# Softmax weights of two heads normalized by one two-tensor multiplication instead of two multiplications with a scalar per row

## The chip, the cores and the metric

The kernel runs on one core of a Trainium2 chip. The metric is the device time of one execution in microseconds (us); three executions of the kernel before are given, and their median counts. The engines are named as in the profile: PE is TensorE (matmuls; PEld its weight loads), DVE is VectorE, ACT is ScalarE, POOL is GpSimd, SP is SyncE (here it issues most DMAs).

## What is computed

The reference is windowed attention followed by two feed-forward stages. For the edit the first matters: scores of each head with a distance bias, a mask (96 local and 8 global positions), a softmax over the row, and the product with the values.

```python
scores = scale * np.matmul(q, k.transpose(0, 1, 3, 2))      # B, H, S, D = 2, 8, 768, 64
scores = scores + bias[None, :, :, :]
scores = np.where(keep, scores, -1000000000.0)
scores = scores - np.max(scores, axis=-1, keepdims=True)
a = np.exp(scores)
a = a / (np.sum(a, axis=-1, keepdims=True) + 1e-09)          # the division that the edit touches
attn = np.matmul(a, v)
h = x @ w_in                                                 # x: 1536 x 512, w_in: 512 x 2048
g = np.where(h > 0.0, h, np.exp(np.minimum(h, 0.0)) - 1.0)
x = g @ w_out
h = np.maximum(np.maximum(x @ w1, x @ w2), x @ w3)           # 512 x 768 each
out = h @ w_out2
```

## The kernel before

**Attention steps.** A step is 128 queries of two heads (`u` = 0, 1, one on each half of PE's rows). There are 48 steps: 6 groups of 256 queries, 4 pairs of heads, 2 halves of a group (`t`). A step sees only a window of keys: 232 columns (96 + 8 + 128), or 128 where it is the first block of a sequence (8 of the 48 steps). The row tile `p` (128 x 512, f32) holds both heads side by side: head 0 in columns 0 to n, head 1 from column 232 on, with n = 232 or 128. The small tile `m` (128 x 8) holds for each head the row's extreme (columns 0, 1), the sum (2, 3), the sum plus 1e-9 (4, 5) and its reciprocal (6, 7).

Step k passes through these stages, each a method called from the loops: `scores_pe` (PE, L217), `scores_dve` (DVE adds the bias and finds the extreme, L243, a custom instruction and the reading of its accumulator for each head), `scores_act` (ACT's exponential with a row sum, L264), `sums` (ACT, L226), `recip` (DVE, L255), `norm` (DVE, L277, the method that is edited), `turn_pe` (PE transposes p in four pieces of 116 columns, or two of 128: L293, L287), `turn_act` (the copy of the transposed tile out of PSUM, L304), `values_pe` (PE, L316), and then a copy or a split of the result (L326, L332, or L352).

**The order of the work** is written out by hand: the queues of the engines run in the order in which the Python loops issue, and semaphores order them against one another. Three parts matter.

- *The head* (`windowed`): steps 0 to 17, one loop turn each. In turn k the order is: scores on PE for k, values for k-3, transposes for k-2; DVE's bias for k; ACT's copies for k-3 and k-2 and exponentials for k, then the sums; DVE's reciprocal and `norm` for k-1; DVE's split remainder (L332) for k-3. From turn 7 on pieces of the conversion of the first weights are put in behind (`c_low` L408, `c_word` L415, `c_rest` L428 on DVE; `c_rebase` L404, `c_high` L423 on ACT): the weights come as 64-bit floats, whose words are put together into an f32, which is split into a rounded part and a remainder.
- *The first feed-forward stage* (`Feed.run`): three blocks of 512 tokens, 16 turns each. A turn multiplies the block with one slice of w_in (`product`, L505, 12 matmuls), takes the activation (ACT L525, L526, DVE L530), splits it (ACT L512; remainder L517 on POOL in block 0, on DVE later) and multiplies with the slice of w_out before (L536, L544). The other 30 attention steps are put into the turns of blocks 0 and 1, one each: PE does the transposes of step k-1 right behind `product`, and on even k then the scores of k and k+1. DVE does `scores_dve`, later `recip` and `norm` of step k. In block 0 the conversion of the next slices of weights stands between these, so `norm` follows a `c_word` (L415) and is followed by `c_rest` (L428).
- *The second stage* (L700 on): three products and a maximum (L725) and the output rows (L569, L574, L579), without attention.

At the change of blocks `run` splits the next tokens (L485 on ACT, L486 on DVE) and saves the finished block (L558).

Of the kernel before, what the change touches and what calls it, by code (L numbers as in the profile page):

```python
# [17 lines left out]
ALU = mybir.AluOpType  # L18
# [5 lines left out]
P = 128  # L24
# [8 lines left out]
WIN = PREV + G + P  # L33
# [75 lines left out]
class Windowed:  # L109
# [159 lines left out]
    def norm(self, k):  # L269
        if k not in self.p_t:  # L270
            return
        nc = self.nc
        n = self.geom(k)[-1]
        p, m = self.p_t[k]
        for u in range(2):
            o = slice(u * WIN, u * WIN + n)
            nc.vector.tensor_scalar(p[:, o], p[:, o], m[:, 6 + u:7 + u], None, op0=ALU.mult)  # L277

    def turn_pe(self, k, tag="TX"):
        if k not in self.p_t:  # L280
# [756 lines left out]
```

## Time and profile before

| | |
|---|---|
| three runs | 569.98, 570.61, 571.79 us, median 570.61 |
| span of the profiled execution, first to last instruction | 569.0 us |
| PE busy | 549.6 us (97%) |
| DVE busy | 315.4 us (55%) |
| ACT busy | 277.1 us (49%) |
| POOL busy | 78.3 us (14%) |
| `norm` (L277), 96 instructions | 28.3 us of DVE |

The span leaves out what the device does ahead of the first instruction and behind the last, so it is a little shorter than a run's time. Busy shares are means over the whole span; the stages have different limits, and a stretch has to be read by itself. A start in the timeline is when the instruction began on its engine; the next one can begin a little before the one ahead has ended, since an engine's pipeline overlaps them. In brackets behind an instruction stands how long its engine had been idle, and what the profile takes for the releaser. "Issue" there means that nothing the profile shows was waited for.

### The profile page before, as it was taken

The page shows a single profiled execution, that of the slowest core. Times are in us where ns is not written, and L with a number is a line of the kernel's source. Part 1 is how long each engine was busy: PE and PEld are TensorE (multiplying, and loading weights), DVE is VectorE, ACT ScalarE, POOL GpSimd, SP SyncE. Part 2 cuts the span into 40 slices and gives each one's busy share as a digit, 9 for nine tenths or more (in the row PEclk, how much of TensorE's full clock was granted, in tenths as well). Part 3 has the DMA queues.
Part 4 walks back from the last instruction along what each step waited for, and adds up shares of the span by engine and source line. Part 5 has one row for each costly group of instructions (what it writes and reads, how often), then busy time and mean ns, then how long its engine had stood idle before and what let it go on. Part 6 is the DMA issues. An engine that isn't in the chain of part 4 may idle for free. (4 is left out here: it accounts for less than half of the span.)

```text
span 569.0 us, 7586 instructions
## 1 busy us (share of the span) xinstructions
PE 549.6 (97%) x2772; PEld 435.0 (76%) x2772; DVE 315.4 (55%) x684; ACT 277.1 (49%) x622; POOL 78.3 (14%) x87
## 2 busy tenths in 40 slices
PE   8799999999999999999999999999999999999995
PEld 6467777776777777778888888888887888888884
DVE  6987999999745333333466656567754112312112
ACT  5988777777656555554555554524323101311011
POOL 4100222222210000000011222023320000000000
PEclk9969999999999999999999999999999999999999
DMA  8919444532211111010013223122302000010002
GB/s 293 381 45 345 166 168 137 181 122 78 67 36 42 42 41 43 20 55 1 0 38 111 88 98 111 37 75 77 117 29 75 1 1 0 8 67 1 0 1 79
DMA packets 16669, 46.61 MB, mean 82 GB/s; under 512 B 1776, under 2 KB 1776, under 8 KB 16624
## 3 DMA queue, kind: packets, MB, share of 16 engines
q1 hardware_dynamic: 15760, 44.47, 22.8%
q10 hardware_dynamic: 864, 1.57, 0.8%
q8 instruction: 24, 0.39, 0.3%
q14 instruction: 21, 0.17, 0.1%
HBM read 42.90 MB, written 3.15 MB: 81 GB/s over the span
## 5 line engine op out<-in xcount | busy, mean ns | idle before, releaser
L505 PE MATMUL h<-xh,w 128*128 128x512 f32 (+1 forms) x536 | 144.5, 391 | 0.8 <-ACT xh L485 0.8
L505 PEld LDWEIGHTS h<-xh,w 128*128 128x128 f32 x536 | 98.1, 188 | 24.5 <-issue 1.8
L536 PE MATMUL y<-gh,w 128*128 128x512 f32 x384 | 98.6, 399 | 0.0
L512 ACT CAST gh<-e 128x512 fp32r<-128x512 f32 x66 | 41.0, 622 | 101.8 <-DVE e L725 87.4
L536 PEld LDWEIGHTS y<-gh,w 128*128 128x128 f32 x384 | 69.7, 188 | 18.1 <-ACT e L526 1.7
L725 DVE TENSOR_TENSOR e<-S,e 128x512 f32<-128x512 f32 x36 | 24.9, 692 | 103.5 <-PE S L505 100.8
L505 PE MATMUL h<-xl,w 128*128 128x512 f32 (+1 forms) x268 | 81.8, 386 | 0.0
L505 PE MATMUL S<-xh,w 128*128 128x512 f32 x288 | 77.0, 389 | 0.0
L530 DVE SCALAR_TENSOR_TENSOR e<-e,h 128x512 f32<-128x512 f32 x48 | 33.0, 687 | 67.7 <-ACT e L526 67.7
L505 PEld LDWEIGHTS S<-xh,w 128*128 128x128 f32 x288 | 54.1, 188 | 11.2
L525 ACT ACTIVATE e<-h 128x512 f32<-128x512 f32 x48 | 28.7, 597 | 65.2 <-PE h L505 63.0
L462 POOL TENSOR_TENSOR w<-wr,w 128x512 fp32r<-128x512 f32 x24 | 35.4, 1474 | 166.1 <-ACT w L461 166.1
L505 PEld LDWEIGHTS h<-xl,w 128*128 128x128 f32 x268 | 50.0, 188 | 10.3
L517 DVE TENSOR_TENSOR gl<-e,gh 128x512 fp32r<-128x512 f32 x50 | 39.8, 796 | 31.8 <-ACT gh L512 31.6
L264 ACT ACTIVATE p<-p,m 128x232 f32<-128x232 f32 (+1 forms) x96 | 44.8, 469 | 24.4 <-DVE m L243 24.4
L544 PE MATMUL y<-gl,w 128*128 128x512 f32 x192 | 51.5, 390 | 0.0
L415 DVE SCALAR_TENSOR_TENSOR wr<-wr 128x1024 uint32<-128x1024 uint32 (+1 forms) x36 | 49.9, 1395 | 0.8 <-ACT wr L404 0.2
L505 PE MATMUL S<-xl,w 128*128 128x512 f32 x144 | 44.3, 389 | 0.0
L451 DVE SCALAR_TENSOR_TENSOR wr<-wr 128x512 uint32<-128x512 uint32 x48 | 43.0, 896 | 2.2
L544 PEld LDWEIGHTS y<-gl,w 128*128 128x128 f32 x192 | 36.0, 188 | 7.9 <-issue 0.3
L569 PE MATMUL y<-w,gh 128*128 128x512 f32 x144 | 37.3, 390 | 0.4 <-POOLq L941 0.4
L517 POOL TENSOR_TENSOR gl<-e,gh 128x512 fp32r<-128x512 f32 x16 | 21.0, 1310 | 104.3 <-ACT gh L512 104.3
(85 smaller groups left out, 604.4 us busy)
## 6 DMA issues: line engine op xcount, KB each, us to landing
wr<-wa SPq DMA_DIRECT2D x14, 1024.0 KB, 6.4
wr<-wb SPq DMA_DIRECT2D x24, 512.0 KB, 3.3
v<-v SPq DMA_DIRECT2D x24, 256.0 KB, 2.8
raw<-qk SPq DMA_DIRECT2D x16, 312.0 KB, 3.1
raw<-qk SPq DMA_DIRECT2D x8, 260.0 KB, 3.3
wr<-wa SPq DMA_DIRECT2D x4, 512.0 KB, 3.8
out<-ot ACTq DMA_DIRECT2D x6, 256.0 KB, 2.6
out<-ot SPq DMA_DIRECT2D x6, 256.0 KB, 2.5
```

The costliest lines, as they stand in the source:

```text
L264: self.nc.scalar.activation(p[:, o], p[:, o], AF.Exp, bias=m[:, u:u + 1], scale=-1.0, accum_out=m[:, 2 + u:3 + u],)
L415: self.nc.vector.scalar_tensor_tensor(r[..., 0], r[..., 1], v, r[..., 0], op0=op, op1=ALU.bitwise_or)
L451: self.nc.vector.scalar_tensor_tensor(t, a, c, t, op0=op, op1=ALU.bitwise_or)
L462: nc.gpsimd.tensor_tensor(w[:, j % 2, 1], v, w[:, j % 2, 0].bitcast(F32), op=ALU.subtract)
L505: nc.tensor.matmul(out[:, o:n], w[:, part % 2, c * P:c * P + P], (xl if part == 2 else xh)[:, c, o:n], start=c == 0 and part == 0, stop=c ...
L512: self.nc.scalar.copy(gh[:, 0:n], e[:, 0:n])
L517: (engine or self.nc.vector).tensor_tensor(gl[:, 0:n], e[:, 0:n], gh[:, 0:n].bitcast(F32), op=ALU.subtract)
L525: self.nc.scalar.activation(e, h, AF.Relu, scale=-1.0)
L530: self.nc.vector.scalar_tensor_tensor(e, e, -1.0, h, op0=ALU.add, op1=ALU.max)
L536: self.nc.tensor.matmul(y[e][:, 0:n], w[:, a, e * P:e * P + P], g[0][:, 0:n], start=fc == 0 and a == 0, stop=False,)
L544: self.nc.tensor.matmul(y[e][:, 0:n], w[:, 0, e * P:e * P + P], g[1][:, 0:n], start=False, stop=fc == NFC - 1,)
L569: nc.tensor.matmul(o[r], gh[:, r * P:r * P + P], w[:, a], start=j == 0 and a == 0, stop=False,)
```

## The change

`norm` no longer multiplies each head's n columns by a scalar per row (the reciprocal of that head in column 6 or 7 of `m`). It makes a view q of p, 128 x 2 x n, over both heads, and a view r of the two reciprocals in which each is repeated n times by a stride of zero, and multiplies q by r in place with one instruction of two tensors. For n = 232 the two heads adjoin, so that q is one run of 464 columns; for n = 128 a gap of 104 columns lies between them.

```diff
     def norm(self, k):
         ...
         p, m = self.p_t[k]
-        for u in range(2):
-            o = slice(u * WIN, u * WIN + n)
-            nc.vector.tensor_scalar(p[:, o], p[:, o], m[:, 6 + u:7 + u], None, op0=ALU.mult)
+        q = p[:, 0:2 * WIN].rearrange("p (u c) -> p u c", u=2)[:, :, 0:n]
+        r = m[:, 6:8].unsqueeze(2).to_broadcast([P, 2, n])
+        nc.vector.tensor_tensor(q, q, r, op=ALU.mult)
```

No other instruction is added, removed or moved on any engine. What the joined instruction changes besides itself is what PE waits for. PE's queue in the head of the program, at step 3 (turn 5), before (the names: y, S and TX are PSUM tiles, raw holds queries and keys, v the values, ident an identity matrix):

```order
L316 MATMUL y_246<-p,v 64x128 [waits DMAHW6_49,Activation_49]
L316 MATMUL y_246<-p,v 64x128
L293 MATMUL y_268<-ident,p 116x128 [waits DVE_49,PE_49]
L293 MATMUL y_268<-ident,p 116x128
L293 MATMUL y_268<-ident,p 116x128 [waits DVE_49]
L293 MATMUL y_268<-ident,p 116x128
L217 MATMUL S_293<-raw 128x128 [waits DMAHW5_49,Pool_49]
```

And the same place of the changed kernel:

```order
L316 MATMUL y_243<-p,v 64x128 [waits DMAHW6_49,Activation_49]
L316 MATMUL y_243<-p,v 64x128
L293 MATMUL y_264<-ident,p 116x128 [waits DVE_49,PE_49]
L293 MATMUL y_264<-ident,p 116x128 x3
L217 MATMUL S_288<-raw 128x128 [waits DMAHW5_49,Pool_49]
```

Before, the first and the third transpose of a step each waited for DVE, that is for the multiplication of head 0 and of head 1. Now the first alone waits, for the one multiplication of both heads.

## Rows read from the trace of the kernel before

**Rows 1.** The page: busy time of each engine, and PE's granted clock in 40 slices

```profile
PE 549.6 (97%) x2772; PEld 435.0 (76%) x2772; DVE 315.4 (55%) x684; ACT 277.1 (49%) x622; POOL 78.3 (14%) x87
...
PEclk9969999999999999999999999999999999999999
```

**Rows 2.** Busy time by stretch: PE, PEld, DVE, ACT, POOL, clock, DMA share, GB/s

```profile
11.13:14.44 3.31, 3.06 (x28) 1.83 (x30) 2.76 (x19) 3.25 (x15) 0.48 (x1) 1.00 1.04 414
14.44:17.74 3.30, 3.05 (x28) 1.82 (x30) 2.76 (x17) 3.23 (x16) 0.00 (x0) 1.00 1.03 389
60.00:150.00 90.00, 86.12 (x466) 64.90 (x464) 82.87 (x155) 70.00 (x144) 24.47 (x19) 1.00 0.38 128
...
180.00:563.00 383.00, 382.23 (x1796) 311.12 (x1795) 168.15 (x306) 142.02 (x283) 37.37 (x28) 1.00 0.13 44
```

**Rows 3.** Groups of DVE by shape: busy us, mean ns, idle before

```profile
L277 DVE TENSOR_SCALAR p<-p,m 128x232 f32<-128x232 f32 x80 | 24.3, 345 | 1.4
...
L486 DVE TENSOR_TENSOR xl<-xraw,xh 128x512 fp32r<-128x512 f32 x8 | 5.2, 686 | 0.2 <-ACT xh L485 0.2
...
L277 DVE TENSOR_SCALAR p<-p,m 128x128 f32<-128x128 f32 x16 | 4.0, 293 | 0.3
...
L157 DVE TENSOR_TENSOR sc<-sc,rel 128x360 f32<-128x360 f32 x1 | 0.5, 526 | 0.0
```

**Rows 4.** Who waited for L277, us in total and times

```profile
  PE TX L293: 3.9, 7
```

**Rows 5.** Timeline of the head: start us, length us, instruction, count

```profile
12.65 0.20 ACT L226 ACTIVATE m<-m 128x2 f32<-128x2 f32 x1
...
13.09 0.59 DVE L277 TENSOR_SCALAR p<-p,m 128x232 f32<-128x232 f32 x2
...
13.60 0.28 DVE L332 TENSOR_TENSOR xl<-TX,xh 128x128 fp32r<-128x128 f32 x1
...
13.71 0.65 PE L293 MATMUL y<-ident,p 128*116 128x128 f32 x4
...
14.39 0.58 ACT L304 COPY p<-y 116x512 f32<-116x512 f32 x1
...
15.96 0.20 ACT L226 ACTIVATE m<-m 128x2 f32<-128x2 f32 x1
```

**Rows 6.** Timeline of the first block, two turns from 84 to 100 us

```profile
88.03 1.96 DVE L415 SCALAR_TENSOR_TENSOR wr<-wr 128x1024 uint32<-128x1024 uint32 x1
...
90.09 0.61 DVE L277 TENSOR_SCALAR p<-p,m 128x232 f32<-128x232 f32 x2
90.58 0.41 PEld L293 LDWEIGHTS TX<-ident,p 128*116 128x116 f32 x4 [0.82 <-issue]
90.61 0.62 PE L293 MATMUL TX<-ident,p 128*116 128x128 f32 x4 [0.42 <-DVE p L277]
...
91.18 1.23 DVE L428 TENSOR_TENSOR w<-wr,w 128x1024 fp32r<-128x1024 f32 x1 [0.47 <-ACT w L423]
...
98.57 0.39 PE L505 MATMUL h<-xl,w 128*128 128x512 f32 x1
...
99.61 0.62 ACT L525 ACTIVATE e<-h 128x512 f32<-128x512 f32 x1
```

**Rows 7.** Timelines of DVE and of PE from 126 to 166 us

```profile
129.45 1.23 DVE L415 SCALAR_TENSOR_TENSOR wr<-wr 128x1024 uint32<-128x1024 uint32 x1
...
149.48 0.62 PE L293 MATMUL TX<-ident,p 128*116 128x128 f32 x4 [0.50 <-DVE p L277]
```

**Rows 8.** Timeline of the change to the second block, 163 to 184 us

```profile
163.29 1.89 DVE L486 TENSOR_TENSOR xl<-xraw,xh 128x512 fp32r<-128x512 f32 x3
...
172.01 1.41 DVE L558 COPY yraw<-y 128x256 f32<-128x256 f32 x4
...
179.37 0.59 DVE L277 TENSOR_SCALAR p<-p,m 128x232 f32<-128x232 f32 x2
179.83 0.41 PEld L293 LDWEIGHTS TX<-ident,p 128*116 128x116 f32 x4 [1.06 <-ACT e L525]
```

## The prediction

> **What bounds the kernel now.** I read the page's busy shares and slices first, then busy time by stretch, then the groups of VectorE (DVE) by shape, and last the timeline around each place where TensorE (PE) waits for a normalized tile. PE is busy 97% of a span of 569.0 us [rows 1]; its matmuls set the end in most of the program. Three stretches differ, and the edit acts in the first two alone. From 180 us on PE is busy 382.23 of 383.00 us [rows 2]: nothing that DVE does there reaches the end while DVE stays ahead. From 60 to 150 us (the first block, where weights are converted beside the matmuls) PE is busy 86.12 and DVE 82.87 of 90.00 us [rows 2]: both are near full, so the waits must be read one by one. In the head (8 to 48 us, attention steps one behind the other) a pair of steps takes 3.30 us, in which ACT is busy 3.23 [rows 2].
>
> The work that is edited is small: 80 multiplications of 128x232 at 345 ns and 16 of 128x128 at 293 ns, 28.3 us of DVE in all [rows 3]. PE's waits on it are listed as 3.9 us in 7 cases [rows 4], and another wait of the same kind, at 179.83, is put down to ACT (below).
>
> **How the old pair behaves.** In the head the pair starts at 13.09, and the next DVE instruction starts at 13.60 [rows 5]: the pair holds DVE for 0.51 us, though each half lasts 0.34, because the second starts before the first has ended. PE does not wait for both halves. Its first weight load for the transposes starts 0.49 us after the pair (90.09 to 90.58), before the pair's end at 0.61 [rows 6]: it was released by head 0 alone. That is 0.34 for the first half and some 0.14 of latency.
>
> **What the joined multiplication costs.** The trace has no TENSOR_TENSOR of 464 elements, and none with a stride of zero; both sides must be bounded. The nearest rows are TENSOR_TENSORs with f32 inputs in SBUF: 128x360 in 526 ns, 128x512 in 686 ns [rows 3], so 1.05 ns for an element more. At 464 this gives 526 + 104 x 1.05 ns = 0.64 us, and at 256 (the steps with 128 columns a head) 0.42 us. A chained TENSOR_TENSOR holds DVE for some 0.09 us less than it lasts (three of 128x512 in a row take 1.89 us together, so 0.60 each between starts, against 0.69 [rows 8, 3]). So the joined one holds DVE for 0.55 us where the pair held it 0.51: 0.04 more in each of 40 steps, and at 256 elements 0.34 against about 0.40 (0.51 less the two shares of 0.05 by which its halves are shorter), 0.06 less in 8 steps. From below: were it to run at the rate of the TENSOR_SCALARs (345 - 293 = 52 ns for 104 elements, 0.5 ns each [rows 3]), it would last about 0.46 us. From above: were the zero stride read at half rate, about 1.1 us. I take 0.64, since a strided row near it is not slow: a SCALAR_TENSOR_TENSOR of 128x1024 that reads every second word takes 1.23 us [rows 7], which the line through the rows of 360 and 512 gives for 1024 elements too (0.69 + 512 x 1.05 ns).
>
> The Trainium skill ("VectorE: DVE Perf Modes", Rules for kernel authors) advises for chained DVE operations: "Minimize op *count*, not sems". By that rule the merge should give something back in each step; by the rows a TENSOR_TENSOR needs twice the time for an element, and this eats what the saved start gives. With the rule alone the DVE term of the sum below would be below nothing instead of 0.1 us; the latency term, which is the larger, would stay.
>
> The larger cost is **latency for PE**: all four transposes now need the joined result. The first weight load can start 0.64 + 0.14 = 0.78 us after the multiplication starts, not 0.49: **0.29 us later wherever PE stands waiting for it**. The third transpose no longer waits by itself; since the four of a step stand 0.11 us apart without a gap when PE is late (from 149.48, 0.62 us for four [rows 7]), that wait costs nothing now and gives nothing.
>
> **Where it reaches the end.**
> (a) Head, 8 to 20 us. Here a loop closes: ACT's sums at 12.65, DVE's reciprocal, pair 13.09, transposes 13.71 to 14.36, ACT's copy 14.39, exponentials from 14.88, next sums of this kind 15.96: 3.31 us [rows 5]. The transposes start 0.62 after the pair; with 0.78 they start 0.16 later, and ACT's copy, which starts as they end, too. There are three such turns before 20 us: 3 x 0.16 = 0.5 us. The steps with 128 columns between them have slack and take nothing.
> (b) Head, 20 to 28 us: weights are converted beside the steps, DVE has no idle time, and two pairs lie on its path before ACT waits for it: 2 x 0.04 = 0.1 us. From 28 to 48 us PE (at the lower clock for about ten us [rows 1]) and ACT set the pace, and the later multiplications are covered by ACT's copies and PE's queue. Without that cover it would be another 6 x 0.04 = 0.2 us.
> (c) First block. DVE and ACT close a loop of their own: DVE's word-building at 88.03 to 89.99, then ACT's rounding L423, then DVE's remainder L428 at 91.18, which waits 0.47 us for ACT [rows 6]. The pair at 90.09 lies in that gap: 0.04 us more is hidden. PE waits 0.42 us for the pair, and will start 0.29 later; but PE's next product ends at 98.96, while ACT's relu of it starts at 99.61, behind ACT's own L404 [rows 6]. So 0.65 us of slack takes the 0.29, and as PE is held to DVE's beat at the next wait, it isn't added up. Cost inside the block: 0.
> (d) Last wait of this block, 149.48 (0.50 us) [rows 7]: behind it PE runs ahead of DVE and ACT, so that its delay stays: +0.3 us.
> (e) The turn to the second block. Here the pair lies right ahead of DVE's four copies at 172.01, behind which the remainder follows that ACT's next tile waits for [rows 8]: +0.04. Then the pair at 179.37 releases PE's weight load at 179.83, 0.46 later, the same signature as above; the view names ACT there (1.06 us), by the nearest event [rows 8]: +0.3 us. After this PE waits for no DVE result on its chain.
>
> Sum: 0.5 + 0.1 + 0 + 0.3 + 0.04 + 0.3 = **1.2 us**. The span of 569.0 becomes 570.2; the median of the runs shown is 570.61, 1.6 us above the span (start and end around it), so the forecast is 571.8 us, +0.2%.
>
> **Rivals.**
> 1. *Absorbed.* ACT in the head may have more slack than the 0.03 us between the transposes' end and its copy, and (d) or (e) may be caught by a later wait of PE for ACT. Then 0.1 to 0.5 us are left: 570.9. For it: many waits of ACT between 20 and 30 us; against: each place was followed to its successor.
> 2. *Carried (slower).* In the first block PE is busy 86.12 of 90.00 us [rows 2] and waits for just this tile in every second iteration, 7 times. If PE were the bound there, each delay would add: 7 x 0.29 = 2.0 us, of which (d) is one, so 1.2 + 1.7 = 2.9 us: 573.5, +0.5%. It decides when the slack of ACT behind PE's product (0.65 us at 99.61) is less than the delay, so from a joined multiplication of about 1.0 us, or if the slack is smaller in the other turns. For it: PE's share; against: no DVE or ACT instruction of that block is put down to PE in its wait.
> 3. *Zero stride read at half rate*: 1.1 us, DVE held 0.5 longer a step. Loop (a) loses 3 x 0.6, (b) 2 x 0.5, (d) and (e) 0.75 each, and DVE in the block begins to exceed the 0.47 us of cover: about +5 to +7 us, 576.5.
> 4. *The clock.* PE's granted clock falls to its lower level (1.2 of 2.4 GHz) for about ten us, in the third slice (28 to 43 us) [rows 1]; ahead of it PE stood idle for more of the time than anywhere later. A slower head leaves PE idle a little more; a second such stretch costs at most half its length, 5 us (574 to 576); if the first moved or went away, up to 3 us would come back (569).
> 5. *The edit brings nothing faster than before by itself.* The best case of the multiplication, 0.46 us, would save DVE 0.1 us in the few steps where DVE is the path, and still delay PE by 0.1 at the others: 570.4.
>
> **How the numbers follow.** A difference of 0.3% (1.7 us) is about what a measurement of this kernel can tell from none. Chances: forecast 0.50 (571.0 to 572.8), absorbed, with 5, 0.22 (570.3 to 571.1), carried 0.15, half rate 0.05, clock 0.08 (0.05 slower, 0.03 faster). Slower by over 0.3% (above 572.3): a quarter of the forecast's own half, most of carried, and the slower parts of 3 and 4: 0.34. Faster (below 568.9): 0.03, rounded to 0.04. Within: 0.62. The range leaves out the faster clock, half rate and a second fall: 570.2 to 573.6.
>
> **What would show it.** The joined row at 0.62 to 0.66 us for 464 elements and 0.41 to 0.44 for 256; PE's first transposes 0.77 us after it wherever PE waits; a pair of head steps at 3.45 instead of 3.30 us; the beat of the first block unchanged (PE's waits at 90.61 and 149.48 lie 58.87 us apart [rows 6, 7]), with PE's waits there no shorter than before; PE's last busy stretch shifted by 1.2 us and equally long. Wrong it would be if the joined row lasted over 0.8 us, if the first block became longer, or if the clock's low stretch had another length.

## The result and the profile after

| | median | runs | spread |
|---|---|---|---|
| before | 570.48 us | 4 | 569.98 to 571.79 |
| changed | 577.32 us | 4 | 573.59 to 580.83 |

The ratio is 1.011 with an interval of 1.0068 to 1.0153: the change is slower, by more than the measurement is uncertain, and the time lies above the predicted range. Twelve more runs of the changed kernel, beside 35 of the kernel before, gave 574.71 against 570.42 us, ratio 1.007 (1.0038 to 1.0101). The changed kernel's runs scatter: the two of them that were traced (578.74 here, 580.15 in experiment 4) show different courses of PE's clock in the first 45 us. A time alone therefore mixes the edit with the clock, and most of what follows compares the start of the same instruction in two traces.

The page of the changed kernel, the lines that answer to [rows 1]:

```profile
PE 553.2 (96%) x2772; PEld 437.2 (76%) x2772; DVE 318.3 (55%) x636; ACT 277.9 (48%) x622; POOL 78.9 (14%) x87
...
PEclk8679999999999999999999999999999999999998
```

PE is busy 3.6 us longer for the same 2772 matmuls. That is the clock: the second slice (14 to 29 us) stands at 6, where before it stood at 9. (With the same course of the clock, in experiment 7, PE is busy 548.0 us with either form.) The groups of DVE, which answer to [rows 3], and PE's waits on L277, which answer to [rows 4]:

```profile
L277 DVE TENSOR_TENSOR p<-p,m 128x464 f32<-128x464 f32 x40 | 26.8, 671 | 1.4
...
L277 DVE TENSOR_TENSOR p<-p,m 128x256 f32<-128x256 f32 x8 | 3.4, 426 | 0.3
```

```profile
  PE TX L293: 7.9, 16
```

DVE spends 1.9 us more on it (30.2 for 28.3). PE's listed waits grow from 3.9 us in 7 cases to 7.9 in 16. To see where the end moved, I took the start of each attention step's first DVE instruction (L243) in both traces, and the difference:

| place | before, us | changed - before |
|---|---|---|
| step 4 (head) | 11.91 | +0.42 |
| step 6 | 15.23 | +2.26 |
| step 10 | 24.75 | +4.21 |
| step 18 (into the first block) | 51.16 | +4.19 |
| step 32 (end of the first block) | 151.41 | +4.39 |
| step 33 | 160.82 | +4.67 |
| step 35 | 177.41 | +4.74 |
| step 39 (second block) | 206.03 | +5.32 |
| step 43 | 234.62 | +5.89 |
| step 47 | 263.21 | +6.47 |
| last output copy ends | 563.30 | +6.73 |

There are three places: the head between 12 and 24 us, the end of the first block (+0.3), and the second block, which loses some 0.14 us a step from 177 us on. In the head the clock does it. Busy time by stretch (columns as in [rows 2]) of the changed kernel:

```profile
8.00:12.00 4.00, 2.79 (x19) 1.78 (x18) 3.41 (x17) 3.48 (x16) 1.45 (x2) 0.84 1.03 399
12.00:16.00 4.00, 4.00 (x24) 2.20 (x22) 2.39 (x13) 3.22 (x14) 0.48 (x1) 0.50 1.04 410
16.00:20.00 4.00, 4.00 (x22) 2.34 (x20) 2.08 (x9) 2.83 (x11) 0.71 (x2) 0.50 1.05 398
20.00:24.00 4.00, 4.00 (x23) 2.29 (x21) 3.00 (x14) 2.85 (x11) 0.42 (x2) 0.50 0.61 232
```

From 12 to 24 us the clock is 0.50, the lower level (1.2 GHz), where before it was 1.00 [rows 2]; by the trace's clock records it is low from 10.74 to 24.4 us. Now PE is busy all of each stretch, where before 28 matmuls filled 3.06 of 3.31 us [rows 2]: PE has become the bound of the head. The timeline there:

```profile
15.62 1.11 PE L293 MATMUL y<-ident,p 128*116 128x128 f32 x4
...
16.76 0.59 ACT L304 COPY p<-y 116x512 f32<-116x512 f32 x1 [0.76 <-PE y L293]
```

Four transposes take 1.11 us (0.65 in [rows 5]) and ACT waits for them. The low stretch costs some 3.7 us: the 4.21 us at step 10 less about 0.5 that the edit itself costs there (experiment 7). Before, one of 10 us lay at 30.3 to 40.6 us, and the changed kernel has one of 6.8 us there too (34.6 to 41.5), so this is an additional one.

The first block keeps its beat. Its timeline, which answers to [rows 6, 7]:

```profile
94.45 0.73 DVE L277 TENSOR_TENSOR p<-p,m 128x464 f32<-128x464 f32 x1
...
95.29 0.41 PEld L293 LDWEIGHTS TX<-ident,p 128*116 128x116 f32 x4 [0.77 <-issue]
95.32 0.62 PE L293 MATMUL TX<-ident,p 128*116 128x128 f32 x4 [0.38 <-DVE p L277]
...
154.16 0.62 PE L293 MATMUL TX<-ident,p 128*116 128x128 f32 x4 [0.51 <-DVE p L277]
```

From 95.32 to 154.16 are 58.84 us; before, the same two transposes stood 58.87 apart [rows 6, 7]. The second block does not keep it. First the timeline of the kernel before:

```profile
193.68 0.59 DVE L277 TENSOR_SCALAR p<-p,m 128x232 f32<-128x232 f32 x2
...
194.14 0.41 PEld L293 LDWEIGHTS TX<-ident,p 128*116 128x116 f32 x4 [0.26 <-issue]
194.17 0.62 PE L293 MATMUL TX<-ident,p 128*116 128x128 f32 x4
...
208.47 0.62 PE L293 MATMUL TX<-ident,p 128*116 128x128 f32 x4
```

And the same place of the changed kernel:

```profile
198.52 0.17 DVE L255 RECIPROCAL m<-m 128x2 f32<-128x2 f32 x1 [1.04 <-ACT m L226]
198.72 0.64 DVE L277 TENSOR_TENSOR p<-p,m 128x464 f32<-128x464 f32 x1
...
199.48 0.41 PEld L293 LDWEIGHTS TX<-ident,p 128*116 128x116 f32 x4 [0.56 <-issue]
199.51 0.62 PE L293 MATMUL TX<-ident,p 128*116 128x128 f32 x4 [0.17 <-DVE p L277]
...
214.09 0.62 PE L293 MATMUL TX<-ident,p 128*116 128x128 f32 x4 [0.16 <-DVE p L277]
...
272.42 0.62 PE L293 MATMUL TX<-ident,p 128*116 128x128 f32 x4 [0.17 <-DVE p L277]
```

PE now waits for the joined result in every second turn, six times between 199 and 273 us, and from one such turn to the next are 14.58 us (199.51 to 214.09) where there were 14.30 (194.17 to 208.47). **The sign of it stood in the trace of before**: the weight load started 0.46 us after the pair, as at 179.83 [rows 8], only with a gap of 0.26 us that the view calls "issue". PE took head 0 there just as it came. With the joined form the load starts 0.76 after the multiplication (198.72 to 199.48), and the loop through PE's product, ACT's relu (L525, L526), DVE (L530), ACT (L512), DVE (L517, L243), ACT's exponentials and sums, and DVE's reciprocal returns each 0.28 to the next turn, as experiment 4 tests.

### The profile page after: what moved, and what is told of

The parts are those of the page before. It is cut to its first block, busy times and chain, and to the rows that moved or that the text cites. A ratio compares the mean times of both kernels' runs of the same rounds, so it can differ in the third digit from the quotient of the medians.

```text
span 576.8 us, 7547 instructions
## 1 busy us (share of the span) xinstructions
PE 553.2 (96%) x2772; PEld 437.2 (76%) x2772; DVE 318.3 (55%) x636; ACT 277.9 (48%) x622; POOL 78.9 (14%) x87
## 5 line engine op out<-in xcount | busy, mean ns | idle before, releaser
L512 ACT CAST gh<-e 128x512 fp32r<-128x512 f32 x66 | 41.0, 622 | 101.4 <-DVE e L725 87.1
L530 DVE SCALAR_TENSOR_TENSOR e<-e,h 128x512 f32<-128x512 f32 x48 | 33.0, 687 | 69.3 <-ACT e L526 69.3
L525 ACT ACTIVATE e<-h 128x512 f32<-128x512 f32 x48 | 28.6, 597 | 65.4 <-PE h L505 63.1
L517 DVE TENSOR_TENSOR gl<-e,gh 128x512 fp32r<-128x512 f32 x50 | 39.7, 795 | 31.8 <-ACT gh L512 31.6
L415 DVE SCALAR_TENSOR_TENSOR wr<-wr 128x1024 uint32<-128x1024 uint32 (+1 forms) x36 | 49.9, 1396 | 0.7
L517 POOL TENSOR_TENSOR gl<-e,gh 128x512 fp32r<-128x512 f32 x16 | 21.0, 1313 | 106.9 <-ACT gh L512 100.9
```

What stands on the lines that cost most here:

```text
L415: self.nc.vector.scalar_tensor_tensor(r[..., 0], r[..., 1], v, r[..., 0], op0=op, op1=ALU.bitwise_or)
L512: self.nc.scalar.copy(gh[:, 0:n], e[:, 0:n])
L517: (engine or self.nc.vector).tensor_tensor(gl[:, 0:n], e[:, 0:n], gh[:, 0:n].bitcast(F32), op=ALU.subtract)
L525: self.nc.scalar.activation(e, h, AF.Relu, scale=-1.0)
L530: self.nc.vector.scalar_tensor_tensor(e, e, -1.0, h, op0=ALU.add, op1=ALU.max)
```

## The experiments

Three explanations are to be told apart. **Theory A**: latency. All transposes wait for the whole result, and each place at which PE took head 0 just in time loses 0.28 us, in the second block in every second turn. **Rival B**: DVE's own time, 642 ns for a pair that held it 0.51. **Rival C**: the clock alone; the edit itself costs about the predicted 1.2 us. The expectations, written before the runs, use one name otherwise: their "theory B" is that the earlier fall of the clock is chance at the start of the program and not the edit's doing, while their theory A counts it as the edit's. That question is taken up in experiment 6.

**1. The joined form in the head alone, and behind it alone.** In the first kernel it is used in the 18 steps of the head:

```diff
-        for u in range(2):
+        if k < 18:
...
+            nc.vector.tensor_tensor(q, q, r, op=ALU.mult)
+        else:
+            for u in range(2):
```

> Joined multiplication in steps 0 to 17 (the head), the pair in steps 18 to 47. Theory A (what the traces before and after suggest: PE's first transposes start 0.3 us later at each place where they wait, which costs about 0.5 us in the head, 0.3 at the end of block 0 and 6 x 0.28 = 1.7 us in block 1; the rest of the loss is PE's clock, which falls in the first turns of the head because PE then stands idle longer): 571.0 us without any more time at the lower clock, and up to 577 with it, scattered over more than 2 us from run to run; two turns of block 1 take 14.30 us as before. Theory B (the earlier fall of the clock is chance at the start of the program, not the edit): 571 us, with clock and scatter of the kernel before (569.98 to 571.79).

Measured: 571.61 us (12 runs, 569.96 to 576.43), ratio 1.0039 (1.0009 to 1.0069). In the trace it is 0.46 to 0.56 us behind the kernel before from step 10 to step 14, near the sum of (a) and (b) of the prediction; from step 16 on it is 0.83 to 0.90 ahead, since the clock did not fall after it had risen (0.82 at the end). So the low stretch of before (30.3 to 40.6 us) costs about 1.4 us. The scatter does not tell the two views of the clock apart: 28 runs of the kernel before, beside it, went from 568.34 to 577.16 us. The second block, with its pairs, has the old beat.

The second kernel is the reverse (`if k >= 18`).

> The pair in steps 0 to 17, the joined multiplication in steps 18 to 47. Theory A: 570.5 + 0.3 + 0.3 + 1.7 = 572.8 us, within 0.8 us from run to run, mean clock 0.989 as before; two turns of block 1 take 14.58 instead of 14.30 us. Theory B: the clock and the scatter of the changed kernel (573.6 to 580.8) in some runs, whatever the head does.

Measured: 574.05 us (11 runs, 571.76 to 580.42), ratio 1.0071 (1.0035 to 1.0106). Against the trace of before: +0.05 at step 31, +0.40 at step 33, +0.44 at step 35, +1.00 at step 39, +2.15 at step 47, +2.47 at the last copy. With the head untouched the loss of the blocks is there, and the second block holds 2.0 of it. Rival C falls: the blocks cost more than twice the whole sum of the prediction, although the low stretch of the clock was shorter than before (6.8 us for 10.2). Two things were not as expected: the median lies 1.2 us above the 572.8, and the runs scatter over 8.7 us instead of 0.8. Runs that far above the others thus come also with the pair in the head.

**2. Head 1 first.** The pair stays, in reverse order, so that DVE's work is the same but the first transposes need the second result:

```diff
-        for u in range(2):
+        for u in (1, 0):
```

> The pair everywhere, but head 1 is multiplied ahead of head 0, so that PE's first transposes wait for the second multiplication, 0.25 us later, while DVE works no longer than before. Theory A (it is the latency): like the changed kernel, 570.5 + 0.4 + 0.3 + 0.2 + 6 x 0.22 = 572.7 us and above it with the clock, up to 579; PE's waits for L277 16 or more instead of 7. Rival (it is the time that DVE is held, or the two-tensor form): 570.5 us as before.

Measured: 574.02 us (12 runs, 572.91 to 579.29), ratio 1.0075 (1.0046 to 1.0105); +0.27 at step 33, +1.23 at step 43, +2.00 at the end, with 14.54 us from turn to turn. Its timeline in the second block:

```profile
194.18 0.59 DVE L277 TENSOR_SCALAR p<-p,m 128x232 f32<-128x232 f32 x2
...
194.89 0.41 PEld L293 LDWEIGHTS TX<-ident,p 128*116 128x116 f32 x4 [0.51 <-issue]
```

The load starts 0.71 after the pair instead of 0.46. No multiplication was joined, and the loss of the second block came back but for 0.04 us in every second turn. This tells A from B: it is when head 0 is ready, not what DVE does. (The view lists 10 waits of PE for L277 here, 6.5 us, not the 16 that were expected; it is the beat that shows the loss.)

**3. More idle matmuls in the head**, to hold the clock: nine of the first steps get four matmuls that nobody uses.

```diff
-FILL = 2, 2
+FILL = 9, 4
```

> The joined multiplication everywhere, and in the first 9 turns of the head 4 idle matmuls on the identity a turn (before: 2 in each of the first 2 turns), to keep PE at work. Theory A: the clock doesn't fall before 20 us, or less often; 570.5 + 2.9 = 573.4 us or up to 1 us more for the idle matmuls, scatter below 2 us, mean clock 0.989 or more. Theory B: like the changed kernel, 573.6 to 580.8.

Measured: 577.35 us (5 runs, 577.14 to 578.45), ratio 1.012 (1.0076 to 1.0164). That is 4 us above the 573.4 that were expected. The five runs do not scatter and the trace's first low stretch starts at 34.88 us, but the filling stands in PE's path (+3.3 us at step 7, at full clock). As a cure it fails. That the scatter of the changed kernel is the clock's fits this, but five runs are too few to show it, since of the changed kernel's 16 runs only four lie over 3.5 us above its fastest.

**4. The changed kernel again, and the second block's loop made shorter.** First the changed kernel as it is.

> The changed kernel once more, beside the kernel before on the same chip, for its scatter. Theory A (+0.5 us in the head, +2.4 us from 149 us on, and in some runs 3.7 us for an earlier stretch at the lower clock): the fastest runs at 572.5 to 573.5, the median 573 to 575, and single runs up to 581. Rival (the first four runs show what the edit always costs): median 577, none below 573.5.

Measured: 574.71 us (12 runs, 573.70 to 580.15). The median is where theory A expected it, so the 577.32 us of the first four runs are not what the edit always costs. The profiled run was the one of 580.15, and it shows a clock that came late. A row of its timeline, and a stretch of busy time:

```profile
17.00 1.11 PE L293 MATMUL y<-ident,p 128*116 128x128 f32 x4
```

```profile
16.00:20.00 4.00, 4.00 (x25) 2.39 (x22) 1.99 (x12) 2.81 (x13) 0.96 (x2) 1.00 1.02 381
```

The transposes run at half speed (1.11 us) and PE is busy throughout, though the clock column says 1.00: the trace has no clock record before 23.96 us, and without one the view shows full speed.

Next, if A holds, anything that starts the loop's end earlier takes the loss away. In the second block DVE's work for the next scores (L243, in `scores_dve`) goes ahead of the remainder (L517, in `low`); once with the pair, once with the joined form:

```diff
+                if late and bi:
+                    at.scores_dve(k)
                 gl = self.low(e, gh, n, nc.gpsimd if bi == 0 else nc.vector)
-                if late:
+                if late and not bi:
                     at.scores_dve(k)
```

> The pair, but in block 1 DVE adds the bias (L243) ahead of the remainder (L517), so that exponentials, sums, reciprocal and multiplication come about 1 us earlier in each turn. Theory A (in block 1 PE's transposes in every second turn start just as the pair is done, with 0.26 us of idle weight load ahead): PE no longer waits there, 6 or 7 x 0.1 to 0.26 = 0.7 to 1.8 us less: 568.3 to 569.4. Rival (PE sets the pace in block 1, and the pair has slack): no difference, 570.0.

> The joined multiplication with the same earlier bias in block 1. Theory A: block 1 takes as long as with the pair in this order, so 0.5 (head) + 0.3 (end of block 0) + 0.1 = 0.9 us more than with the pair, some 569.2 to 570.3 in the fast runs, 2 to 3 us below the changed kernel; two turns of block 1 take the same time with pair and joined. Rival (the loss in block 1 has another cause than when the tile is ready): 1.7 us or more above the pair in this order.

Measured: 568.99 us with the pair, ratio 0.998 (0.9951 to 1.0009), and 570.90 with the joined form, ratio 1.0017 (0.9979 to 1.0055), 12 runs each. The two traces have the same course of the clock. The joined one is 1.34 us behind at step 32, 1.59 at step 33 and 1.63 at steps 36, 39, 43, 47 and at the last copy: **the second block's loss is gone**, and the rest remains. Why, shows the timeline of the joined one:

```profile
192.60 0.64 DVE L277 TENSOR_TENSOR p<-p,m 128x464 f32<-128x464 f32 x1
...
194.01 0.40 PE L505 MATMUL h<-xl,w 128*128 128x512 f32 x1
194.02 0.59 PEld L293 LDWEIGHTS TX<-ident,p 128*116 128x116 f32 x4
```

The result is there 0.78 us before PE gets to it (193.24 to 194.02), and both kernels go from turn to turn in 14.24 us. That is 0.06 us less than the pair needed in the old order (14.30), so even the pair had nothing to spare there. The rest, 1.63 us, is more than the 0.9 that were expected; 1.11 of it lie ahead of step 18.

**5. The filling made small.** Two idle matmuls a step in steps 8 to 12 too, with the pair and the loop of experiment 4:

```diff
-            if k < FILL[0]:
+            if k < FILL[0] or 8 <= k < 13:
                 f.fill(at.ident, FILL[1])
```

> The pair with the earlier bias of block 1, and two idle matmuls a turn in turns 8 to 12 of the head, where PE stands idle for 1 to 2 us a turn (18 to 30 us). If PE's idle time there is what lets the clock fall at 30 us, that stretch goes: 1.4 us less than the pair in this order, 567 to 568, mean clock 0.995 or more. If not, the same as the pair in this order or up to 1 us slower.

> Joined multiplication with the earlier bias of block 1 and the idle matmuls in turns 8 to 12, beside the same with the pair (568.0 us median, 567.4 the fastest). Theory A: the head's and the block borders' 1.6 us stay: fastest 569.0, median 569.6 to 570; low stretch of the clock at 30 us gone or shorter. Rival (the head's loss is only the clock's): 568.0.

Measured: 568.01 us with the pair, ratio 0.9958 (0.9924 to 0.9992), and 569.66 with the joined form, ratio 0.9991 (0.9957 to 1.0025). The joined form's median stays 1.7 us behind, as in experiment 4 (1.9); the two traces differ in their clock, so they do not settle where. Two runs of the pair and four of the joined form lie 4 to 6 us above the fastest. Three of these six have a granted clock of 0.982 to 0.985 on record, the other three 0.998 and 0.999, as a late clock without a record, like that of the 580.15 above, would leave it. So three more idle matmuls go ahead of the first step (`WARM = 11` for 8), with the pair:

> The pair with the earlier bias, the idle matmuls in turns 8 to 12, and 11 instead of 8 idle matmuls at the start of the program. If the slowest runs (5 us above the others) are those in which PE's clock stays low from the start to 24 us, and more work at the start lets it rise, they go: 567.4 to 569 us in all runs. If not: 568.0 us with 1 or 2 of 12 runs near 573, as with 8.

Measured: 567.95 us, ratio 0.9932 (0.9903 to 0.9962), all 12 runs within 567.47 to 569.04. **This one beats both kernels.** Its clock on the page:

```profile
PEclk9999999999999999999999999999999999999998
```

**6. Does the joined form bring the late clock?** The joined form in the eight steps of 128 columns alone (`if n == P`), the first step among them, where PE's first transposes now come at 9.4 instead of 8.9 us.

> The joined multiplication in the 8 steps with 128 columns a head alone, the pair in the other 40. Where PE waits it waits for tiles of 232 columns, except once at 8.9 us. Theory A: 0 to 0.2 us more than before, 570.4 us, DVE 0.06 us less busy in each of the 8 steps; block 1 at 14.30 us for two turns. Rival (the form with a stride of zero costs more than its rows show, wherever it stands): 0.5 us or more above before.

Measured: five of 12 runs at 570.4 to 572.0 us, near the 570.4 expected, and seven at 575.0 to 577.8, which were not expected; median 575.35, ratio 1.0056 (1.0018 to 1.0093). In its profiled run (571.47) all blocks stand 0.3 us ahead of before, but its low stretch of the clock is the shorter one (6.8 for 10.2 us); beside the pair of experiment 7, at the same course of the clock, it is 0.2 to 0.4 us behind from step 14 on. Read with the others: of the kernels with eight idle matmuls at the start and the joined form in the head, 23 of 64 runs lie over 3.5 us above the fastest of their kernel, of those with the pair 31 of 164. Experiment 3's filled kernel is left out of this (none of 5); without the kernel of this experiment it is 16 of 52. That would suit an edit that raises the chance of a late clock, but the kernel before has such runs too (22 of 117), the shares of single kernels go from 2 in 12 to 7 in 12, and most of these runs were not traced. It **stays open** whether the edit raises the chance.

**7. Both forms at an equal clock.** The eleven idle matmuls, once with the joined form, once with the pair, and nothing else:

```diff
-WARM = 8
+WARM = 11
```

> The changed kernel with 11 instead of 8 idle matmuls at the start, nothing else. If the changed kernel's runs of 577 to 581 us are those in which PE's clock is low for most of the first 24 us, and the idle matmuls let it rise in time: 573.5 to 575 us in 11 or 12 of 12 runs, median 574.3, so 3.5 to 4.2 us above the pair with the same start. If the edit brings on the low clock whatever stands ahead: 2 to 5 of 12 runs stay above 577.

> The kernel before with 11 instead of 8 idle matmuls at the start. Median 570.2 us, and none of its runs at 573 to 577, where one in five of the kernel before lies; the difference to the changed kernel with the same start is then the cost of the edit without the clock's chance: 0.6 in the head, 0.4 + 0.3 at the block borders, 2.1 in block 1, 3.4 us in sum (theory A); 1.2 us if block 1 is as the prediction had it.

Measured: 574.97 us joined (10 runs, 573.41 to 577.01), 570.18 with the pair (12 runs, 568.95 to 571.70); ratios 1.0072 (1.0041 to 1.0103) and 0.9996 (0.9974 to 1.0018). The pair came out as expected. The joined form's median is 0.7 us above its expectation, and five of its ten runs lie above the 575 that all but one were to stay below. In the two traces the clock has the same course, with one low stretch of 6.8 us from 28.4 and from 28.6 us. So their difference up to the last output copy is the edit:

| place | joined - pair, us | gained there |
|---|---|---|
| step 10 | +0.44 | head |
| step 18 | +0.65 | head, 0.65 in all |
| step 21 | +0.94 | first block, once |
| step 31 | +0.97 | first block, 0.32 in all |
| step 33 | +1.32 | last wait of the first block, 0.35 |
| first transposes of the second block, 180 us | +1.67 | 0.35 |
| last ones of it, 268 us | +3.34 | six further turns, 1.67 |
| last output copy | +3.36 | nothing from 268 us on |

Rows behind the last three lines, of the pair:

```profile
179.26 0.63 PE L293 MATMUL TX<-ident,p 128*116 128x128 f32 x4 [0.69 <-ACT e L525]
...
562.14 0.58 ACT L745 COPY ot<-y 128x512 f32<-128x512 f32 x1 [0.77 <-PE y L574]
```

And of the joined form:

```profile
180.93 0.62 PE L293 MATMUL TX<-ident,p 128*116 128x128 f32 x4 [0.97 <-DVE p L277]
...
268.42 0.62 PE L293 MATMUL TX<-ident,p 128*116 128x128 f32 x4 [0.16 <-DVE p L277]
...
565.50 0.59 ACT L745 COPY ot<-y 128x512 f32<-128x512 f32 x1 [0.77 <-PE y L574]
```

The spans differ by 4.4 us (568.1 and 572.5), of which about 1.0 lies behind the last output copy. That stretch is 5.0 us long in one kernel with the joined form (experiment 1, head), 5.8 in another (experiment 4), 6.4 to 6.8 in the changed kernel and here, and 6.6 with the reversed pair of experiment 2, so it does not go with the joined form alone. Where it comes from is not settled.

## Why the prediction was wrong

**The price of the instruction: right.** The joined row has a median of 642 ns for 464 elements and 426 for 256; 0.64 and 0.42 were predicted. It holds DVE for 0.56 us (9.86 to 10.42 us in experiment 7's joined trace; 0.55 predicted). A stride of zero costs nothing that shows here, and rival 3 falls. The strided row that the prediction leaned on was a weak support, though: L415 of 128x1024 takes 1.23 us in one place [rows 7] and 1.96 in another [rows 6].

**The latency: right, but for the first block.** In the head and the second block PE's first weight load starts 0.76 us after the multiplication (0.78 predicted), 0.30 later than behind the pair. Where PE waits in the first block it starts 0.84 after (94.45 to 95.29), 0.36 later than behind the pair: these rows last 0.73 us instead of 0.64. All seven of them in experiment 7's joined trace overlap one of POOL's multiplications (L187).

**(a) and (b), the head: the sum is near, its parts are not.** At equal clock it is 0.65 us against 0.6 (experiment 7). Of this 0.47 is there by step 11, at 27 us. It then shrinks to 0.38 at step 17, and the rest comes from PE's waits at 46 and 48 us, where the prediction counted on cover: the transposes start 0.79 us after the multiplication there, and 0.49 after the pair. That the parts add up to the forecast is in part luck, and in experiment 4 the head costs 1.11 us.

**(c), the first block: nearly.** The beat is unchanged, but the block took 0.32 us once, nearly all of it at one turn near its start; "0" was wrong by that. The timeline of the joined form of experiment 7:

```profile
69.03 1.18 ACT L404 ACTIVATE wr<-wr 128x1024 f32<-128x1024 f32 x1
...
69.59 0.39 PE L505 MATMUL h<-xl,w 128*128 128x512 f32 x1
...
70.36 0.60 ACT L525 ACTIVATE e<-h 128x512 f32<-128x512 f32 x1 [0.15 <-issue]
...
71.73 0.69 DVE L530 SCALAR_TENSOR_TENSOR e<-e,h 128x512 f32<-128x512 f32 x1 [0.27 <-ACT e L526]
```

The same place with the pair (experiment 7):

```profile
68.57 0.39 PE L505 MATMUL h<-xl,w 128*128 128x512 f32 x1
...
69.44 0.59 ACT L525 ACTIVATE e<-h 128x512 f32<-128x512 f32 x1
```

With the joined form ACT is idle ahead of its relu for 0.15 us, and DVE then waits 0.27 us for ACT; in the pair's trace neither gap is there. The relu starts 0.38 us after PE's product has ended (69.98 to 70.36); with the pair it is 0.48 (68.96 to 69.44), behind ACT's L404. So this turn took up 0.10 of the 0.36 us and passed the rest on. The prediction had read 0.65 us of slack at 99.61 [rows 6] and let it stand for all turns. Why the relu did not start sooner is not shown: in the next such turns of the same trace it starts 0.16 to 0.48 us after the product (from 85.03 to 85.19 in the first), the delay is taken up, and the block runs on DVE's beat again. Rival 2 had named this case, a slack that is smaller in other turns.

**(d), the last wait of the first block: right**, 0.35 us (0.3 predicted). **(e), the first wait of the second block: right** too, 0.35 us, and the signature of 0.46 us was rightly read as head 0, against the releaser that the view named.

**The step that failed is the last sentence of (e)**: "After this PE waits for no DVE result on its chain". I looked there for waits that the view names as DVE's, and for a span full of PE work [rows 2]. Neither shows a case in which PE takes a tile with nothing to spare. The same signature stood at 194.14 of the trace of before, and in every second turn behind it. Six turns of 0.28 us are 1.67 us, the largest term of the whole edit at equal clock, and the prediction had put it at nothing. A stretch of 382.23 busy in 383.00 us says that PE waits little, not that there is slack ahead of it. Rival 2 had this mechanism and even its price, 7 x 0.29 = 2.0 us; it was put into the first block, where DVE's beat absorbs it, instead of the second, where PE is the bound and the delay is carried.

**The clock (rival 4) had too small a chance.** It was named with up to 5 us, and the changed kernel's profiled run lost 3.7 us by it. But it was thought of as something that the edit might cause; about one in five of the runs of the kernel before lies over 3.5 us above its fastest, which three runs of before could not show. At an equal clock the edit costs 3.36 us to the last copy and 4.8 us between the medians (experiment 7), which would have been some 575 us, still above the range. Of the 1.4 us between these two numbers 1.0 lies behind the last output copy in the traces, and its cause is not settled. What lies between 575 and the 577.32 of four runs goes with the clock: the run of 573.59 had a mean granted clock of 0.993, the other three 0.980 to 0.987. Only the run of 578.74 was traced.

## What to carry to other kernels

Two instructions joined into one deliver both results when the last one is done: whoever took the first half just in time is late by as much as the joined instruction lasts longer than the first half (0.30 us here), and if it stands on a loop, in every turn. Look for such places by the distance from the producer's start to the consumer's, in each stage by itself, also where the view names no wait or says "issue": a distance at its smallest value is a consumer with no slack. And compare two kernels by the start of the same instruction in traces with the same clock, since a median of a few runs mixes the two.

## What the runs showed of the hardware

- The clock's course at the start of the program differs between runs of one kernel. With eight idle matmuls ahead of the first step it fell again at 10.74 us in one run of the changed kernel and came up only at 24 us in another; with eleven (PE busy with them from 0.98 to 5.37 us in the pair's trace of experiment 7) none of 24 runs with the pair, and one of ten with the joined form, lay over 3.5 us above the fastest of its kernel. The three more cost no time that shows (570.18 us against 569.94 of before).
- Before the first clock record the profile shows full speed, also where PE ran at half (experiment 4). Four transposes of 1.11 us instead of 0.62 to 0.65 tell the lower level.
- Joined multiplications of 464 elements lasted 0.64 to 0.65 us wherever no POOL instruction overlapped them, and every one over 0.66 us (up to 0.89) overlapped POOL's L187. That POOL is the cause was not tested.
- The TENSOR_TENSOR with a stride of zero takes the time of one without it here (642 ns for 464 elements; 526 for 360 and 686 for 512 without [rows 3]), and two chained TENSOR_SCALARs hold DVE shorter than the one TENSOR_TENSOR (0.51 against 0.56 us): one instruction less saved nothing.
